# A W1 pair fetched ahead of the last WO rows and summed later, and a third attention block fetched ahead of the last x^T tiles, in a fused attention and MLP layer

## The chip, the cores and the metric

One core of a Trainium2 chip runs the whole program. The metric is the device time of one execution in microseconds (us). The kernel before took 1103.58 us (median of 3 runs, 1101.91 to 1105.1).

## The reference

`x` has 2048 rows of 576 numbers. After a layer norm without gain, an attention branch and an MLP branch read the same rows, and both are added to `x`:

```
xn = layernorm(x)
q, k, v = split(xn @ wqkv)                  # 32 heads of 18
logits = (q . k at s, s-2, ..., s-14) * 18 ** -0.5   # 8 keys, masked below row 0
A = (softmax(logits) @ v) @ wo              # wo: 576 x 576
B = maximum(xn @ w1, 0) @ w2                # w1: 576 x 4608, w2: 4608 x 576
return x + A + B
```

Everything is float32.

## The kernel before, in words

**Numbers.** Each matrix operand is split in two parts, a high part (`hi`, written by ScalarE) and a low part (`lo`, the difference, written by VectorE or GpSimd), and TensorE adds three products, hi*hi, hi*lo and lo*hi. The split is what most ScalarE and VectorE instructions do (`two`, L169, L171, L173; `ot_split`, L722 to L724; `xt_parts`, L429 to L435).

**Phases and groups.** The rows are worked on in two phases (even rows, then odd rows), each with four tiles of x^T of 256 rows (`XT[ph, 0..3]`). W1 has 36 blocks of 128 columns. Two blocks form a pair; for each pair and each two x^T tiles there is one group `g` (30 groups in phase 0, whose first 6 blocks are done in the opening, 36 in phase 1). A group multiplies 2 x 2 blocks by seven products (Strassen's scheme in Winograd's form, `M`, L1011), so sums of W1 blocks are needed (`sw_mix`, L977) and sums of x^T tiles (`ts_steps`, L444 to L470). The hidden values go through the ReLU (`c_parts`, L812 and L816) and are multiplied with W2 (`o_half`, tile `po`).

**Steps.** `group` is written out by hand as eight steps. A step gives TensorE one set of paired products and one half of an output piece. The events tied to a step are fired in its middle (`"T"`) or at its end (`"O"`); `on(ph, g, i, "O", f)` ties `f` to step `i`. Each engine takes its instructions strictly in the order written: one that waits holds up all that stand behind it on that engine. Within a group, step 2 copies bank `a` to bank `q` (`seed`, ScalarE L1045, tile `ph<-ph`), and TensorE needs that bank in step 4 (the rows `ph<-xS` that follow `pm<-xT`).

**W1.** For pair `p`, whose first group is `a = 2p`, `sw_load` (L965, L970, SyncE) fetches the four blocks into the staging tile `st` in step 4 of group `a - 2`, after the last splits of the pair before it have read `st`. Three sums (`sw_mix`) come in step 8 of `a - 2` and steps 1 and 2 of `a - 1`, the fourth in step 4, on VectorE in phase 1. The splits (`sw_prep`) follow from step 5 on.

**Where attention ends.** Attention is VectorE work spread over the groups, four units of eight heads a phase. The last unit's result goes to DRAM (`o_out`, L647, `od<-att`). Then the projection with WO needs: the last two of five groups of WO rows (`wo_rest`, L264 and L267, `att<-wo`), which land in the tile `att` that `od<-att` has just been read from; the four blocks of rows of the attention output (`ot_in`, L713 and L715, `att<-od`, block `r` = 0 to 3); and their splits (`ot_split`). These steps stand in a list (`ot_plan`) of entries with a condition and with ages in modelled TensorE time of earlier entries; `ot_go` takes the first entry that is ready, at places written in the groups. `ot_go(ph, r)` takes entries until block `r` is split.

**The seam.** `seam` joins the phases: `tail_pieces` ends phase 0's last group, and `more(k)` in it fetches the last x^T tiles of phase 1 (`xt_in`, L402 and L404, `xT<-words`, tiles 2 and 3); then blocks 0 and 1 are multiplied with WO (`wo_half`, L139, `po<-wq,att`), with the preparation of phase 1 taken from the list `side`. Blocks 2 and 3 are multiplied in the gaps of phase 1's first group (`prologue` and `wo_fill`). In phase 1, `epilogue` does the projection after the last group.

Of the kernel before, what the change touches and what calls it, by code (L numbers as in the profile page):

```python
# [66 lines left out]
def tile_body(ctx: ExitStack, tc: tile.TileContext, x, wqkv, wo, w1, w2, out):  # L67
# [14 lines left out]
    NP = [(NF - f) // 2 for f in F0]  # L82
    NG = [2 * n for n in NP]
# [39 lines left out]
    t = {"pe": 0.0, "dve": 0.0}  # L123
# [88 lines left out]
    def w2_load(ph, f):  # L212
        z = W2S[ph, f] = st2.tile([P, D], F32, name="st2")
        nc.sync.dma_start(z, w2[f * P : (f + 1) * P, :])
# [60 lines left out]
    hold = {}  # L275
# [124 lines left out]
    def words_in(z, td):  # L400

        nc.sync.dma_start(z[:, 0:KT], td[0 : KT * P].rearrange("(k p) t -> p k t", p=P))  # L402
        for part in LOW, UPP:
            nc.sync.dma_start(z[part, KT], td[KT * P : D])  # L404
# [14 lines left out]
    def xt_in(ph, tb):  # L419
        d = XT[ph, tb] = xtp.tile([P, 10, TBN], F32R, name="xT")  # L420
        words_in(f32(d[:, 0:5, :]), TD.pop((ph, tb)))
# [134 lines left out]
    ready = {}  # L556
# [545 lines left out]
    def on(ph, g, i, z, f, *a):  # L1102
        if g < 0:
            ph, g = ph - 1, g + NG[ph - 1]
        evs[ph, g, i, z].append((f, a))
# [5 lines left out]
    def plan_strassen(ph):  # L1111
        for p in range(NP[ph]):
            a = 2 * p
            f = F0[ph] + 2 * p
            engine = nc.vector if p > 1 or ph else nc.gpsimd
            if p or ph:
                on(ph, a - 2, 4, "O", sw_load, ph, p)
                for k, (d, i) in enumerate(((-2, 8), (-1, 1), (-1, 2)) if p > 1 or ph else ((-1, 3),) * 3):
                    on(ph, a + d, i, "O", sw_mix, k, engine)
                on(ph, a - 1, 4, "O", sw_mix, 3, engine)  # L1120
                on(ph, a - 1, 5, "T", sw_prep, ph, p, "A11")
                on(ph, a - 1, 5, "O", sw_prep, ph, p, "S2")
                on(ph, a - 1, 7, "T", sw_prep, ph, p, "S1", "A12")
                if p:
                    on(ph, a, 2, "O", sw_prep, ph, p, "S3", "S4")
                    on(ph, a, 3, "T", sw_prep, ph, p, "A22", "rem")
                if p:
                    on(ph, a - 1, 5, "O", w2_load, ph, f)
                    on(ph, a - 1, 6, "O", w2_load, ph, f + 1)
                on(ph, a, 6, "T", w2_split, ph, f, (0,), True)  # L1130
                on(ph, a, 8, "T", w2_split, ph, f, (1,), True)
                on(ph, a + 1, 1, "O", w2_split, ph, f + 1, (0,))
                on(ph, a + 1, 3, "O", w2_split, ph, f + 1, (1,))
        for u, g in QKV_G[ph].items():
            on(ph, g - (3 if u else 2), 4, "O", wq_load, ph, u)
            for kt, (d, i) in enumerate(((-2, 4 if u else 8), (-2, 7 if u else 8), (-1, 1), (-1, 4), (-1, 6))):
                on(ph, g + d, i, "O", wq_split, ph, u, kt)
            for tb in range(NTB):
                a, i = g + tb // 2, 3 + 4 * (tb % 2)
                ins[ph, a, i].append((qkv_half, (ph, u, tb, False, True)))  # L1140
                ins[ph, a, i + 1].append((qkv_half, (ph, u, tb, True, True)))
            on(ph, g + 2, 1, "T", halos, ph, u)
            on(ph, g + 2, 1, "T", attention, ph, u)
            if u:
                on(ph, g + 2, 4, "T", attention_rest, ph, u)
            else:
                on(ph, g - 2, 6, "O", zero_row, ph, K_ROW)
                on(ph, g - 1, 2, "O", zero_row, ph, V_ROW[0])
        g = QKV_G[ph][NU - 1] + 2
        on(ph, g, 1, "O", wo_first, ph)  # L1150
        on(ph, g + 1, 5, "O", wo_split, ph, 0)
        on(ph, g + 3, 3, "O", wo_split, ph, 1)
        on(ph, g + 5, 3, "O", wo_split, ph, 2)
        g = NG[ph] - 1
        if ph:
            on(ph, g, 5, "O", hold.__setitem__, ("xs", ph), True)
            on(ph, g, 1, "O", last_room, ph)
        else:
            on(ph, g, 4, "O", last_room, ph)
            on(ph, g, 4, "O", xt_in, 1, 0)  # L1160
            on(ph, g, 4, "O", hold.__setitem__, ("go", 0), True)
            on(ph, g, 4, "O", ot_go, 0)
            on(ph, g, 5, "O", xt_in, 1, 1)
            on(ph, g, 5, "O", hold.__setitem__, ("go", 1), True)
            for i in (6, 7, 8):
                on(ph, g, i, "O", ot_go, 0)

# [2 lines left out]
    def ot_plan(ph):  # L1170
        z = OTQ[ph] = []
        done = lambda: ph in ready and t["pe"] > ready[ph] + 4.5
        free = lambda: done() and ("xs", ph) in hold

        def go(r):
            if ph:
                return free if r == 3 else done
            return lambda: done() and ("go", r) in hold

        z.append(("wl", wo_rest, (ph,), lambda: ph in ready and t["pe"] > ready[ph] + 4.0, ()))  # L1180
        for kt in range(3, KT + 1):
            z.append((("ws", kt), wo_split, (ph, kt), None, (("wl", 11 + 3.0 * (kt - 3)),)))
        for r in range(4):
            z.append((("in", r), ot_in, (ph, r), go(r), ((("in", r - 1), 3.0),) if r else (("wl", 2.0),)))
            for h in range(2):
                z.append((("split", r, h), ot_split, (ph, r, h), None, ((("in", r), 12.0),)))

    def ot_go(ph, need=None):
        z = OTQ.get(ph, [])
        if need is not None:  # L1190
            todo_now = [("split", need, 0), ("split", need, 1), ("ws", KT)]
            while any((ph, k) not in OTT for k in todo_now):
                assert ot_one(ph, z, False), (ph, need)
            return
        ot_one(ph, z, True)

    def ot_one(ph, z, timed):
        for e in z:
            name, f, a, when, after = e
            if when is not None and not when():  # L1200
                continue
            if any((ph, k) not in OTT or timed and OTT[ph, k] + d > t["pe"] for k, d in after):
                continue
            z.remove(e)
            f(*a)
            OTT[ph, name] = t["pe"]
            return True
        return False
# [183 lines left out]
    def aside(n):  # L1392
        for _ in range(min(n, len(side))):
            f, *a = side.popleft()
            f(*a)

    def tail_pieces(ph, more, then):
        g = NG[ph] - 1
        tail_end(ph, more, lambda: (then(), o_half(ph, g, 2, False)))
        then()  # L1400
        own_banks(g, 3, ps_m, "pm", D - 256)
        o_half(ph, g, 3, False)
        then()
        for piece in (2, 3):
            o_half(ph, g, piece, True)
            o_evict(ph, g, piece)

    def sums(tp):
        side.extend([(ts_run, 1, tp, 1)] * 4)
        for i in range(4 * tp, 4 * tp + 4):  # L1410
            side.extend([(xt_parts, 1, i, 0), (xt_parts, 1, i, 1)])
        side.extend([(low_twin, 1, 2 * tp)] + [(ts_run, 1, tp, 1)] * 4)

    def seam():

        def more(k):
            ot_go(0)
            if k > 1:
                xt_in(1, k)

        tail_pieces(0, more, lambda: ot_go(0))
        hold["go", 2] = True
        for i in range(2):
            w2_load(1, i)
        sums(0)
        side.extend([(sw_prep, 1, 0, "S3", "S4"), (sw_prep, 1, 0, "A22", "rem")])
        for r in range(2):
            for k in range(4):
                ot_go(0, r) if k == 0 else ot_go(0)
                wo_half(0, r, k % 2, k > 1)  # L1430
                aside(3)
                if k == 2:
                    ot_go(0, r + 1)
            if r == 0:
                hold["go", 3] = True
        sums(1)
# [109 lines left out]
    late(22, sw_prep, 0, 0, "S3", "S4")  # L1546
    late(23, sw_prep, 0, 0, "A22", "rem")
    plan_strassen(0)
    plan_strassen(1)
    ot_plan(0)  # L1550
    ot_plan(1)

    both, x_low, w_low, last = TERMS[0:4], TERMS[4:8], TERMS[9:13], [TERMS[8], TERMS[13]]
# [92 lines left out]
    for n in range(FIRST, NOLD - 2):  # L1646
        g = n - n % 2 + LAG
# [17 lines left out]
    for g in range(1, NG[0]):  # L1665
        group(0, g)
    seam()
    prologue(1, wo_fill)
    for g in range(1, NG[1]):
# [29 lines left out]
```

## Time and profile before

| | before |
|---|---|
| runs, median (lowest to highest) | 1103.58 us (1101.91 to 1105.1) |
| profiled execution | 1107.0 us |
| its span, first to last instruction | 1105.2 us |
| TensorE (PE) busy | 1092.0 us, 99% |
| VectorE (DVE) busy | 844.1 us, 76% |
| ScalarE (ACT) busy | 590.8 us, 53% |
| GpSimd (POOL) busy | 274.1 us, 25% |
| moved by DMA | 179.62 MB, mean 163 GB/s |
| granted TensorE clock, mean | 0.997 |

The profile is one execution. A row of its timeline reads: start in us from the span's start, length in us, engine, line of the kernel, operation, tile written and tile read, shape, count; in brackets how long the engine had been idle before it, and what ended that. SPq rows are SyncE's DMA issues. A row of the chain of waits reads: who waited, for whom, us in total, times, longest. A row of busy time by stretch gives the stretch, its length, busy time of PE, PEld (weight loads), DVE, ACT and POOL, then the granted clock, the mean busy share of the 16 DMA engines and what they moved in GB/s. A row of DMA issues gives tiles, queue, count, KB each and the median us from issue to landing.

### The profile page before, as it was taken

How to read it: one execution, taken by the hardware profiler on the slowest of the kernel's cores; microseconds unless marked ns; L12 is line 12 of the kernel's file. 1: busy time of each engine (PE TensorE's matmuls, PEld its weight loads, DVE VectorE, ACT ScalarE, POOL GpSimd, SP SyncE). 2: the span in 40 equal slices, each digit the busy share in tenths (PEclk: the TensorE clock that was granted, in tenths of full speed). 3: DMA queues.
4: the chain of work that ended last, by engine and by line, in shares of the span. 5: the costliest groups of instructions: out<-in, count | busy, mean ns of one | idle time of the engine just before them, and what ended most of it. 6: DMA issues, size and time to landing. Idle time of an engine off the chain costs nothing.

```text
span 1105.2 us, 37855 instructions
## 1 busy us (share of the span) xinstructions
PE 1092.0 (99%) x16338; PEld 1081.9 (98%) x16338; DVE 844.1 (76%) x1402; ACT 590.8 (53%) x1396; POOL 274.1 (25%) x267
## 2 busy tenths in 40 slices
PE   9999999999999999999999999999999999999898
PEld 8999999999999999999999999999999999999898
DVE  7676888897997988893763297988889798896521
ACT  5433563564466366565774466356356446655640
POOL 2311521222222223322231122223022222223121
PEclk9999999999999999999999999999999999999899
DMA  7469995696597598889966597499579569888886
GB/s 231 138 163 226 189 195 95 147 207 108 122 223 132 90 219 158 157 157 259 239 139 122 107 205 142 76 218 172 91 157 205 101 132 205 155 165 177 192 135 149
DMA packets 138806, 179.62 MB, mean 163 GB/s; under 512 B 28032, under 2 KB 85120, under 8 KB 138608
## 3 DMA queue, kind: packets, MB, share of 16 engines
q0 software_dynamic: 38720, 83.76, 48.2%
q1 hardware_dynamic: 99200, 92.55, 29.4%
q8 instruction: 129, 2.11, 0.7%
q10 hardware_dynamic: 720, 0.89, 0.2%
q14 instruction: 37, 0.30, 0.1%
HBM read 74.07 MB, written 98.58 MB: 156 GB/s over the span
## 4 chain that ended last, share of the span: by engine, by line
PE 93%; DMA 4%; DVE 1%; SPq 1%; issue 1%; ACT 0%; POOL 0%; DVEq 0%; POOLq 0%; ACTq 0%
PE po L160 35%; PE po L139 19%; PE ph L160 18%; PE pm L160 14%; PE pm L139 2%; DMA st<-in_w 2%; PE ph L139 2%; PE ph L127 1%; DMA xT<-words 1%; PE po L127 1%; DMA att<-od 1%; SPq L398 1%; PE po L116 0%; PE pm L351 0%; DVE att L416 0%
## 5 line engine op out<-in xcount | busy, mean ns | idle before, releaser
L160 PE MATMUL po<-ar 64*128 64x256 f32 (+1 forms) x6240 | 498.4, 289 | 0.0
L160 PEld LDWEIGHTS po<-ar 64*128 64x128 f32 x6240 | 435.3, 184 | 0.4 <-PE ph L160 0.4
L160 PE MATMUL ph<-xT,ar 64*128 64x256 f32 x2772 | 348.8, 274 | 0.2 <-DVE ar L816 0.2
L160 PEld LDWEIGHTS ph<-xT,ar 64*128 64x128 f32 x2772 | 314.7, 185 | 0.7 <-DVE ar L816 0.4
L771 POOL DMA_DIRECT2D out<-ev x131 | 157.4, 1202 | 547.4 <-ACT ev L765 408.3
L160 PE MATMUL pm<-xS,ar 64*128 64x256 f32 x2376 | 282.5, 274 | 0.0
L160 PEld LDWEIGHTS pm<-xS,ar 64*128 64x128 f32 x2376 | 259.7, 184 | 0.3
L765 ACT ACTIVATE ev<-po 128x512 f32<-128x512 f32 (+1 forms) x272 | 176.8, 652 | 115.5 <-PE po L160 83.1
L173 DVE TENSOR_TENSOR ar<-st,ar 128x256 fp32r<-128x256 f32 (+3 forms) x244 | 128.9, 548 | 46.8 <-ACT ar L169 46.3
L139 PE MATMUL po<-wq,xT 64*128 64x432 f32 x1512 | 156.4, 354 | 0.0
L169 ACT ACTIVATE ar<-st 128x256 fp32r<-128x256 f32 (+3 forms) x314 | 150.6, 500 | 4.9 <-DMA st<-in_w 2.7
L139 PEld LDWEIGHTS po<-wq,xT 64*128 64x128 f32 x1512 | 138.4, 184 | 4.6
L160 PE MATMUL ph<-xS,ar 64*128 64x256 f32 x792 | 113.5, 277 | 6.1 <-ACT ph L1045 6.1
L160 PEld LDWEIGHTS ph<-xS,ar 64*128 64x128 f32 x792 | 104.9, 186 | 6.8 <-ACT ph L1045 6.6
L171 POOL TENSOR_TENSOR ar<-st,ar 128x256 fp32r<-128x256 f32 (+1 forms) x70 | 75.9, 1085 | 143.5 <-ACT ar L169 101.8
L618 DVE TENSOR_TENSOR pr<-att 128x1152 f32<-128x1152 f32 x64 | 88.3, 1392 | 0.4
L583 DVE TENSOR_TENSOR pr<-att 128x1152 f32<-128x1152 f32 x64 | 87.0, 1369 | 0.1
L586 DVE TENSOR_REDUCE att<-pr 128x64 f32<-128x1152 f32 x64 | 85.8, 1344 | 0.0
L977 DVE TENSOR_TENSOR st<-st 128x256 f32<-128x256 f32 x128 | 62.6, 490 | 14.9 <-DMA st<-in_w 14.7
L541 ACT ACTIVATE att<-po 128x288 f32<-128x288 f32 (+1 forms) x88 | 28.7, 403 | 81.2 <-PE po L139 81.2
L625 DVE TENSOR_TENSOR pr<-pr 128x1152 f32<-128x1152 f32 x64 | 69.2, 1082 | 1.4
L160 PE MATMUL pm<-xT,ar 64*128 64x256 f32 x396 | 67.5, 276 | 0.1
(131 smaller groups left out, 1218.5 us busy)
## 6 DMA issues: line engine op xcount, KB each, us to landing
out<-ev POOLq DMA_DIRECT2D x131, 576.0 KB, 7.1
st<-in_w SPq DMA_DIRECT2D x72, 288.0 KB, 5.2
st<-in_w SPq DMA_DIRECT2D x69, 256.0 KB, 3.7
att<-att SPq DMA_DIRECT2D x16, 441.0 KB, 4.6
att<-in_wqkv SPq DMA_DIRECT2D x28, 216.0 KB, 6.8
od<-att SPq DMA_DIRECT2D x32, 160.0 KB, 6.5
st<-in_w SPq DMA_DIRECT2D x66, 64.0 KB, 6.4
att<-in_x SPq DMA_DIRECT2D x14, 288.0 KB, 4.1
```

Source lines behind the costliest of these rows:

```text
L139: ins = nc.tensor.matmul(o, l[z], r[z], start=start, stop=stop)
L160: b.ins = nc.tensor.matmul(b.ap, l[part], r[part], start=start, stop=stop, skip_group_check=skip)
L169: nc.scalar.activation(hi, src, AF.Copy)
L171: nc.gpsimd.tensor_tensor(lo, src, f32(hi), op=ALU.subtract)
L173: nc.vector.tensor_tensor(lo, src, f32(hi), op=ALU.subtract)
L583: nc.vector.tensor_tensor(pr[i], q, window(k, i), op=ALU.mult)
L586: nc.vector.tensor_reduce(lg[:, i], pr.pop(i).rearrange(heads, d=Dh), axis=AX.X, op=ALU.add)
L618: nc.vector.tensor_tensor(pr[i].rearrange(heads, d=Dh), e, window(v, i).rearrange(heads, d=Dh), op=ALU.mult)
L625: nc.vector.tensor_tensor(o, z[:, :, 0:n], z[:, :, n : 2 * n], op=ALU.add)
L765: nc.scalar.activation(acc[:, :, cols], z[:, :, 0 : cols.stop - cols.start], AF.Copy)
L771: ADDED[ph, tb] = nc.gpsimd.dma_start(rows_of(ph, tb), acc, accum_op=ALU.add)
L977: engine.tensor_tensor(stg(o), stg(a), stg(b), op=op)
```

## The change

```
             if p or ph:
                 on(ph, a - 2, 4, "O", sw_load, ph, p)
-                for k, (d, i) in enumerate(((-2, 8), (-1, 1), (-1, 2)) if p > 1 or ph else ((-1, 3),) * 3):
+                if (ph, p) in ((1, 0), (1, NP[1] - 1)):
+                    on(ph, a - 2, 4, "O", hold.__setitem__, ("wl", 1 if p else 0), True)
+                apart = p and a + 2 < NG[1] if ph else p > 1
+                for k, (d, i) in enumerate(((-2, 8), (-1, 1), (-1, 2)) if apart else ((-1, 3),) * 3):
                     on(ph, a + d, i, "O", sw_mix, k, engine)
...
             on(ph, g, 5, "O", hold.__setitem__, ("go", 1), True)
+            on(ph, g, 6, "O", hold.__setitem__, ("go", 2), True)
...
-        z.append(("wl", wo_rest, (ph,), lambda: ph in ready and t["pe"] > ready[ph] + 4.0, ()))
+        z.append(("wl", wo_rest, (ph,), lambda: ph in ready and t["pe"] > ready[ph] + 4.0 and ("wl", ph) in hold, ()))
...
-            z.append((("in", r), ot_in, (ph, r), go(r), ((("in", r - 1), 3.0),) if r else (("wl", 2.0),)))
+            z.append((("in", r), ot_in, (ph, r), go(r), ((("in", r - 1), 6.0 if ph else 3.0),) if r else (("wl", 2.0),)))
...
             if k > 1:
                 xt_in(1, k)
+            if k == 3:
+                ot_go(0, 0)
 
         tail_pieces(0, more, lambda: ot_go(0))
-        hold["go", 2] = True
```

Only in phase 1's first and last pair do the first three W1 sums move: all three now stand in step 3 of group `a - 1`. The WO rows of a phase wait, in the order of the program, until that pair's load has been written. In phase 1 the blocks of attention rows are written at least 6 us of modelled time apart instead of 3. In phase 0 block 2 may be fetched from step 6 of the last group on, and block 0 is split by the end of `more(3)`.

SyncE at the end of attention in phase 1, before: `st` is the W1 staging tile, `wo2` the WO rows, `od` the attention output in DRAM, `st2` W2 rows.

```order
L647 DMA od_12469<-att_11326 32x5x256 x4
L264 DMA att_20292<-wo2_143 128x576
L267 DMA att_20292<-wo2_143 64x1x576 x2
L965 DMA st_82<-in_w1 128x2x256 x2
L970 DMA st_82<-in_w1 64x2x128 x2
L713 DMA att_20292<-od_12469 128x4x256
```

The same place now:

```order
L647 DMA od_12469<-att_11326 32x5x256 x4
L965 DMA st_82<-in_w1 128x2x256 x2
L970 DMA st_82<-in_w1 64x2x128 x2
L264 DMA att_20354<-wo2_143 128x576
L267 DMA att_20354<-wo2_143 64x1x576 x2
L713 DMA att_20354<-od_12469 128x4x256
```

The W1 load has moved ahead of the two WO issues that stood between it and `od<-att`. (In phase 0 it stood ahead of them already.)

VectorE at the same place, before: `u3` and `m5` are sums of the hidden values of the group before, `st` the W1 sums.

```order
L1054 TENSOR_TENSOR u3_20448<-u3_20448,pm_20276 128x256
L977 TENSOR_TENSOR st_82<-st_82 128x2x128
L1054 TENSOR_TENSOR m5_20387<-m5_20387,ph_20257 128x256
L816 SCALAR_TENSOR_TENSOR ar_72<-u3_20448,ar_72 128x256
L816 SCALAR_TENSOR_TENSOR ar_72<-m5_20387,ar_72 128x256
L173 TENSOR_TENSOR ar_72<-st2_20148,ar_72 128x256
L977 TENSOR_TENSOR st_82<-st_82 128x2x128 x2
```

And now:

```order
L1054 TENSOR_TENSOR u3_20448<-u3_20448,pm_20276 128x256
L1054 TENSOR_TENSOR m5_20384<-m5_20384,ph_20257 128x256
L816 SCALAR_TENSOR_TENSOR ar_72<-u3_20448,ar_72 128x256
L816 SCALAR_TENSOR_TENSOR ar_72<-m5_20384,ar_72 128x256
L173 TENSOR_TENSOR ar_72<-st2_20148,ar_72 128x256
L173 TENSOR_TENSOR ar_72<-st2_20148,ar_72 128x320
L977 TENSOR_TENSOR st_82<-st_82 128x2x128 x3
```

The first sum no longer stands between `u3` and `m5`; all three stand behind the W2 splits. The end of phase 0 changes in the same way.

SyncE at the seam, before: `words` holds x^T in DRAM; the first four rows are x^T tiles 2 and 3, then come two W2 rows, and the last two rows are block 2 (block 1 stands just ahead of this piece).

```order
L402 DMA xT_10458<-words_1801 128x4x256
L404 DMA xT_10458<-words_1801 64x256 x2
L402 DMA xT_10475<-words_2160 128x4x256
L404 DMA xT_10475<-words_2160 64x256 x2
L214 DMA st2_10573<-in_w2 128x576
L214 DMA st2_10575<-in_w2 128x576
L713 DMA att_10055<-od_1876 128x4x256
L715 DMA att_10055<-od_1876 64x1x256 x2
```

And now, with block 2 in the first two rows (block 1 still just ahead of them):

```order
L713 DMA att_10055<-od_1876 128x4x256
L715 DMA att_10055<-od_1876 64x1x256 x2
L402 DMA xT_10461<-words_1801 128x4x256
L404 DMA xT_10461<-words_1801 64x256 x2
L402 DMA xT_10478<-words_2160 128x4x256
L404 DMA xT_10478<-words_2160 64x256 x2
L214 DMA st2_10576<-in_w2 128x576
L214 DMA st2_10578<-in_w2 128x576
```

Block 2 is now issued ahead of x^T tiles 2 and 3 and of two W2 rows; block 3 (not shown) stays behind them.

## The prediction

> **What bounds the kernel now.** I read the page first, then who TensorE waits for, then its timeline at those waits, then the engines behind them.
>
> ```profile
> PE 1092.0 (99%) x16338; PEld 1081.9 (98%) x16338; DVE 844.1 (76%) x1402; ACT 590.8 (53%) x1396; POOL 274.1 (25%) x267
> ```
>
> TensorE is the bound; only its waits, and the clock lost in them, can be won. The chain of waits:
>
> ```profile
> PE ph L160 <- ACT ph L1045: 6.1, 2, 4.8
> PE po L139 <- DVE att L723: 0.6, 2, 0.4
> ```
>
> Two waits for the copy into bank `q` make up 6.1 us, one of them 4.8. TensorE's timeline around it:
>
> ```profile
> 1012.30 0.28 PE L160 MATMUL pm<-xT,ar 64*128 64x256 f32 x1
> ...
> 1023.98 0.28 PE L160 MATMUL pm<-xT,ar 64*128 64x256 f32 x1
> 1029.07 0.58 PE L160 MATMUL ph<-xS,ar 64*128 64x256 f32 x1 [4.81 <-ACT ph L1045]
> ...
> 1043.23 0.28 PE L160 MATMUL pm<-xT,ar 64*128 64x256 f32 x1
> ```
>
> The `pm<-xT` rows are step 4 of three groups in a row. The first interval is 11.68 us, an undisturbed group; the second is 19.25. This group loses 7.57 us: the wait, and a slow stretch behind it. The busy time by stretch shows why (granted clock third from the end):
>
> ```profile
> 1028.00:1029.00 1.00, 0.00 (x0) 0.00 (x0) 0.85 (x3) 0.98 (x4) 0.00 (x0) 0.50 1.12 316
> ...
> 1034.00:1035.00 1.00, 1.00 (x18) 1.00 (x18) 0.85 (x2) 0.67 (x2) 0.00 (x0) 0.81 0.92 232
> ```
>
> The clock had fallen to 0.50 in the wait and came back only after 1034. So 7.57 - 4.81 = 2.76 us is the price of the clock. VectorE, then ScalarE:
>
> ```profile
> 1011.52 1.29 DVE L173 TENSOR_TENSOR ar<-st,ar 128x512 fp32r<-128x512 f32 x2 [1.34 <-ACT ar L169]
> ...
> 1019.44 0.42 DVE L1054 TENSOR_TENSOR u<-u,pm 128x256 f32<-128x256 f32 x1 [2.35 <-ACT u L1049]
> 1027.23 0.43 DVE L977 TENSOR_TENSOR st<-st 128x256 f32<-128x256 f32 x1 [7.37 <-DMA st<-in_w]
> 1027.57 0.41 DVE L1054 TENSOR_TENSOR m<-m,ph 128x256 f32<-128x256 f32 x1
> ```
>
> ```profile
> 1028.02 0.42 ACT L812 ACTIVATE ar<-m 128x256 fp32r<-128x256 f32 x1 [7.70 <-DVE m L1054]
> ...
> 1028.65 0.36 ACT L1045 ACTIVATE ph<-ph 128x256 f32<-128x256 f32 x1
> ```
>
> VectorE sits 7.37 us on the first W1 sum (L977); `m` behind it is late, ScalarE's L812 waits for `m`, and the copy that TensorE needs stands behind L812. SyncE shows why the load was late:
>
> ```profile
> 1008.12 1.81 SPq L647 DMA_DIRECT2D od<-att  x4
> 1016.97 0.34 SPq L264 DMA_DIRECT2D att<-wo  x1
> ...
> 1018.63 1.76 SPq L965 DMA_DIRECT2D st<-in_w  x2
> 1020.44 1.31 SPq L970 DMA_DIRECT2D st<-in_w  x2
> ```
>
> ```profile
> SPq L264 <- DMA od<-att: 6.9, 1, 6.9
> ```
>
> The WO issue waits 6.9 us for `od<-att` to be out of the tile, and the W1 load waits behind it though `st` was free from 1012.81, when the splits at 1011.52 ended.
>
> **The change part by part.**
>
> *Load and sums of the last pair.* The load is now directly behind `od<-att` and can go at 1012.85 instead of 1018.63, 5.8 us earlier. Its price in time to land is best read where the same order already stood, at the end of phase 0 (first issue of `st` at 497.67):
>
> ```profile
> 497.67 1.15 SPq L965 DMA_DIRECT2D st<-in_w  x2
> ...
> 507.64 0.43 DVE L977 TENSOR_TENSOR st<-st 128x256 f32<-128x256 f32 x1 [3.85 <-DMA st<-in_w]
> ```
>
> It was there by 507.6, 9.9 us after the first issue: here 1022.8. The sums now stand in step 3, which TensorE leaves at 1023.98, and behind a split that ScalarE feeds; so I expect no wait. Were the load a few us late, `u`, `m`, their ReLU parts and the copy stand ahead of it; behind the sums stand a ReLU part wanted four steps on (some 5.8 us by 11.68 / 8 a step) and the splits for the group that starts after 1030. Two covers for one wait: I take all 7.57 us, with a lower end of 4.81 if a new wait shorter than 2.76 us comes behind.
>
> *Sums of the first pair.* At the end of phase 0 only the sums move. TensorE there:
>
> ```profile
> 496.22 0.28 PE L160 MATMUL pm<-xT,ar 64*128 64x256 f32 x1
> ...
> 496.91 0.94 PE L160 MATMUL po<-ar 64*128 64x256 f32 x12
> ...
> 507.90 0.28 PE L160 MATMUL pm<-xT,ar 64*128 64x256 f32 x1
> ...
> 510.17 0.94 PE L160 MATMUL po<-ar 64*128 64x256 f32 x12
> ```
>
> Step 4's products took 0.69 us in the one group and 2.27 in the next: 1.58 us lost. VectorE now reaches the sums as the load lands (507.6); nothing that TensorE needs soon stands behind. Gain 1.58 us, lower end 0.
>
> *Block 2 at the seam.* TensorE's first half of block 2 lies between the first two of these rows; the next two enclose an undisturbed half of the same width:
>
> ```profile
> 542.21 0.28 PE L160 MATMUL ph<-xT,ar 64*128 64x256 f32 x1
> ...
> 546.33 0.27 PE L160 MATMUL pm<-xS,ar 64*128 64x256 f32 x1
> ...
> 549.09 0.28 PE L160 MATMUL ph<-xT,ar 64*128 64x256 f32 x1
> ...
> 551.32 0.28 PE L160 MATMUL ph<-xS,ar 64*128 64x256 f32 x1
> ```
>
> 4.12 us against 2.23, of which 0.11 is for one pair of products more: 1.78 us lost. It waits for the splits, and those for data:
>
> ```profile
> 514.51 1.38 SPq L713 DMA_DIRECT2D att<-od  x1
> ...
> 530.06 0.38 SPq L713 DMA_DIRECT2D att<-od  x1
> ```
>
> ```profile
> 542.63 1.36 ACT L722 ACTIVATE att<-att 128x640 fp32r<-128x640 f32 x2 [0.15 <-DMA att<-od]
> ```
>
> ```profile
> att<-od SPq DMA_DIRECT2D x1, 512.0 KB, 12.0
> ```
>
> Block 2 was issued at 530.06, 15 us after block 1, and landed 12.0 us later. Now it follows block 1, at about 517; even at 12.0 us it lands by 530. Its two splits go in among the x^T splits and the cuts of `xS`, which ScalarE and VectorE then finish one or two splits (0.7 and 1.0 us each) later; by my count of these rows VectorE ends the second split 0.6 us before TensorE wants it. Gain 1.78, lower end 0; 0.4 us off for that thin margin. Block 0's earlier split costs nothing: it lies ahead of evictions that wait for TensorE anyway. The passed tiles and W2 rows come under the rivals.
>
> *Wider spacing and later WO rows in phase 1.* Both are wanted only behind the last group, in the epilogue; I price them at nothing unless the WO rows hold ScalarE (below).
>
> *Sum.* 7.57 + 1.58 + 1.78 - 0.4 = 10.5 us against the profiled 1107.0: 1096.5. That execution is 3.4 us above the median of the runs, 1103.58. If the runs lose as much as it did, the median becomes 1093.1; if their 3.4 us less is a smaller loss, they end where it would, at 1096.5. I take 1094.0, nearer the first: start and end differ between executions as well.
>
> The end of phase 0 shows what a short wait does to the clock:
>
> ```profile
> 508.00:509.00 1.00, 0.18 (x4) 0.00 (x0) 0.85 (x4) 0.57 (x2) 0.00 (x0) 1.00 1.06 228
> ```
>
> It stayed at 1.00 in a wait of 1.3 us. The Trainium skill, "TensorE: Matmul & The Clock Gate", section on the HAM clock gate, puts the step to half rate after an idle window of about 3.4 us and the step back after about 3.4 us of work. The trace agrees on the first (TensorE stops at 1024.26, 0.50 by 1028) and not on the second (over 5 us of slow work from 1029.07); by the page the clock would cost 1.7 us and not 2.76, and the sum 9.4.
>
> **The rivals.**
>
> *The runs lose less.* Their spread of 3.2 us is about the clock's price. Where the wait is under about 3 us the clock stays: at most 3 + 1.58 + 1.78 = 6.4 us are to be won, 1097.2. For it: the profiled execution is the longest of all. Against: the load is issued 5.8 us late in every run.
>
> *WO rows hold ScalarE.* They now queue behind the W1 load.
>
> ```profile
> att<-wo SPq DMA_DIRECT2D x1, 288.0 KB, 8.3
> ```
>
> In phase 0, in this order, they took 8.3 us: here landed at 1025.3, just as ScalarE comes to their split in step 5. Behind it stand evictions of `po` that TensorE wants within a step or so. Each us beyond some 1027 costs one, and past 3 the clock's 2.76: landing at 1034, 17 us after issue, gives back 5.5 + 2.76 and leaves 1101.3, no change. Against: none of the rows is that slow.
>
> *Slower: x^T tile 3 comes too late.*
>
> ```profile
> xT<-words SPq DMA_DIRECT2D x1, 512.0 KB, 15.0
> ...
> 522.97 2.39 SPq L404 DMA_DIRECT2D xT<-words  x2
> ...
> 545.49 1.29 DVE L470 TENSOR_TENSOR pr<-xT 128x512 f32<-128x512 f32 x2
> ...
> 520.00:525.00 5.00, 5.00 (x72) 4.82 (x72) 1.07 (x2) 1.64 (x4) 1.20 (x1) 1.00 1.12 273
> ```
>
> Block 2, 640 KB at 273 GB/s, is 2.3 us of transfer put ahead of tiles 2 and 3. Tile 3's issues end at 525.4; at 15.0 us each the last rows land between 538 and 540, say 539, and it is wanted at 545.49: 6.5 us to spare. Less 2.3, and 3.4 for a TensorE that is earlier there, leaves 0.8. Past that VectorE holds, in L470, everything for phase 1's first groups. To end slower by 0.3%, 10.5 + 3.3 us must go, so 11 us of wait plus the clock: tile 3 would have to take 27 us; then 1107. For it: the engines are full here (share 1.12).
>
> The Trainium skill, "DMA: Bandwidth & Descriptors", section on queues, rings and completion order, speaks for this case: all of SyncE's transfers use one ring per DMA engine and are taken in ring order, so the moved block holds up all that it passes, by its whole length. That is the 2.3 us, and not 11.
>
> **How the numbers follow.** The forecast, all three waits gone, 1091 to 1096: 0.62. Smaller loss in the runs, 1096 to 1099.5: 0.26. WO rows late, no change: 0.07. Tile 3 late, slower: 0.05. The range 1091.0 to 1099.0 leaves out the last two and little more. 0.3% is 3.3 us, about what a measurement of this kernel can tell from no change; so faster (below 1100.3) 0.88, same 0.07, slower 0.05.
>
> **What would show it.** Right: L977's 7.37 us wait gone, SyncE's W1 issue near 1013 and ahead of WO, the clock 1.00 through the end of phase 1, group intervals of 11.68 us there, no wait of `po` L139 for L722 or L723 after block 1, and a profiled time near 1096.5. Wrong: a new wait of TensorE of over 1 us in the last two groups or the seam, ScalarE waiting for `att<-wo`, VectorE's L470 waiting for `xT<-words`, or a median above 1099 with all three waits gone.

## The result, and the profile after

The changed kernel took 1096.31 us (median of 6 runs, 1095.38 to 1096.8) beside 1103.62 us for the kernel before (6 runs, 1101.91 to 1106.48): ratio 0.9929, 95% interval 0.9915 to 0.9942, so 7.3 us faster. The profiled execution after took 1096.31 us, where the one before took 1107.0: 10.7 us less. Why one difference is 7.3 and the other 10.7 is the main question of what follows.

The span and the busy times, and who TensorE still waits for (total, times, longest):

```profile
span 1094.5 us, 37854 instructions
...
PE 1088.3 (99%) x16338; PEld 1078.5 (99%) x16338; DVE 845.2 (77%) x1402; ACT 590.1 (54%) x1396; POOL 273.0 (25%) x267
```

```profile
PE po L116 <- POOL mhalf L111: 1.4, 1, 1.4
PE ph L127 <- ACT xT L356: 0.7, 1, 0.7
PE pm L160 <- ACT u L1049: 0.2, 1, 0.2
```

The first two rows are the start of the program. The 6.1 us for the copy (L1045) and the waits of `po` (L139) for the attention splits are gone; in their place stands one wait of 0.2 us.

**End of attention in phase 1.** TensorE in step 4 of three groups, then the busy time by stretch (clock third from the end):

```profile
1009.24 0.28 PE L160 MATMUL pm<-xT,ar 64*128 64x256 f32 x1
...
1020.92 0.28 PE L160 MATMUL pm<-xT,ar 64*128 64x256 f32 x1
...
1032.60 0.28 PE L160 MATMUL pm<-xT,ar 64*128 64x256 f32 x1
```

```profile
1024.00:1029.00 5.00, 5.00 (x86) 5.00 (x84) 3.83 (x8) 4.61 (x12) 0.00 (x0) 1.00 1.09 294
1029.00:1036.00 7.00, 7.00 (x120) 7.00 (x119) 5.21 (x12) 5.41 (x13) 2.33 (x2) 1.00 1.04 256
```

Both intervals are 11.68 us, TensorE is busy without a gap and the clock stays at 1.00: the 19.25 us group is an ordinary one. The row at 1009.24 answers to the one at 1012.30 before: 3.06 us had been won by then, and 7.57 more came here. SyncE, how long its W1 loads took to land, and VectorE:

```profile
1005.05 1.79 SPq L647 DMA_DIRECT2D od<-att  x4
1009.18 2.47 SPq L965 DMA_DIRECT2D st<-in_w  x2
1011.71 1.92 SPq L970 DMA_DIRECT2D st<-in_w  x2
1014.41 0.35 SPq L264 DMA_DIRECT2D att<-wo  x1
```

```profile
st<-in_w SPq DMA_DIRECT2D x2, 256.0 KB, 7.3
...
st<-in_w SPq DMA_DIRECT2D x2, 64.0 KB, 7.2
```

```profile
1022.22 0.49 DVE L173 TENSOR_TENSOR ar<-st,ar 128x320 fp32r<-128x320 f32 x1 [2.86 <-ACT ar L169]
1022.63 1.33 DVE L977 TENSOR_TENSOR st<-st 128x256 f32<-128x256 f32 x3
1023.89 0.41 DVE L816 SCALAR_TENSOR_TENSOR ar<-pm,ar 128x256 fp32r<-128x256 f32 x1
```

The load goes 4.1 us after `od<-att`, ahead of WO. The rows on landing give the median of two pieces; the last piece alone, issued at 1012.36, took 7.1 us and was there at about 1019.5, so the sums at 1022.63 had some 3 us to spare and waited for nothing.

**End of phase 0 and seam.** TensorE's step 4 in the group that had lost time, then its first half of block 2; SyncE's issue of block 2 and the time it took to land; VectorE's second split of it:

```profile
507.72 0.28 PE L160 MATMUL pm<-xT,ar 64*128 64x256 f32 x1
...
508.40 0.84 PE L160 MATMUL po<-ar 64*128 64x256 f32 x12
...
540.69 0.28 PE L160 MATMUL ph<-xT,ar 64*128 64x256 f32 x1
...
541.38 1.46 PE L139 MATMUL po<-wq,att 64*128 64x256 f32 x22
...
543.04 0.28 PE L160 MATMUL pm<-xS,ar 64*128 64x256 f32 x1
```

```profile
518.13 0.37 SPq L713 DMA_DIRECT2D att<-od  x1
```

```profile
att<-od SPq DMA_DIRECT2D x1, 512.0 KB, 11.8
```

```profile
539.22 0.68 DVE L723 TENSOR_TENSOR att<-att 128x512 fp32r<-128x512 f32 x1
539.94 0.29 DVE L724 TENSOR_TENSOR att<-att 64x128 fp32r<-64x128 f32 x1
```

Step 4 takes 0.68 us where it took 2.27, block 2's half 2.35 where it took 4.12. Block 2's large piece lands at 529.9; VectorE ends its second split at 540.23, 1.15 us before TensorE begins the half at 541.38.

### The profile page after: what moved, and what is told of

Same layout as the page of the kernel before. It is cut to its first block, busy times and chain, and to the rows that moved or that the text cites. A ratio compares the mean times of both kernels' runs of the same rounds, so it can differ in the third digit from the quotient of the medians.

```text
span 1094.5 us, 37854 instructions
## 1 busy us (share of the span) xinstructions
PE 1088.3 (99%) x16338; PEld 1078.5 (99%) x16338; DVE 845.2 (77%) x1402; ACT 590.1 (54%) x1396; POOL 273.0 (25%) x267
## 4 chain that ended last, share of the span: by engine, by line
PE 97%; ACT 1%; DMA 1%; DVE 0%; issue 0%; POOL 0%; DVEq 0%; ACTq 0%; POOLq 0%; SPq 0%
PE po L160 36%; PE po L139 21%; PE ph L160 18%; PE pm L160 15%; PE pm L139 2%; PE ph L139 2%; PE ph L127 1%; PE po L127 1%; DMA st<-in_w 1%; PE po L116 0%; PE pm L351 0%; ACT ar L169 0%; DVE st L977 0%; PE pm L127 0%; ACT ev L765 0%
## 5 line engine op out<-in xcount | busy, mean ns | idle before, releaser
L160 PE MATMUL po<-ar 64*128 64x256 f32 (+1 forms) x6240 | 492.1, 288 | 0.0
L160 PEld LDWEIGHTS po<-ar 64*128 64x128 f32 x6240 | 429.0, 184 | 0.5 <-PE ph L160 0.4
L139 PE MATMUL po<-wq,xT 64*128 64x432 f32 x1512 | 156.6, 354 | 0.0
L139 PEld LDWEIGHTS po<-wq,xT 64*128 64x128 f32 x1512 | 138.4, 184 | 4.8 <-ACT ev L765 0.2
```

Of the source, the lines that this page charges most:

```text
L139: ins = nc.tensor.matmul(o, l[z], r[z], start=start, stop=stop)
L160: b.ins = nc.tensor.matmul(b.ap, l[part], r[part], start=start, stop=stop, skip_group_check=skip)
```

## The experiments

Each run is compared with runs of the kernel before on the same chip. Those came in three sets, with medians of 1106.7 (34 runs), 1106.2 (20) and 1106.9 us (17), against 1103.6 in the first comparison. The executions of one kernel differ among themselves, on each of the three chips on which the sets were taken. All 71, by mean granted clock, beside the 6 of the changed kernel:

| mean granted clock | runs | mean, us | lowest to highest |
|---|---|---|---|
| before, 1.000 | 12 | 1101.8 | 1101.1 to 1102.4 |
| before, 0.998 | 18 | 1103.9 | 1101.9 to 1106.9 |
| before, 0.997 | 26 | 1107.4 | 1104.6 to 1110.0 |
| before, 0.995 | 15 | 1108.9 | 1107.5 to 1111.2 |
| after, 0.999 and 1.000 | 6 | 1096.1 | 1095.4 to 1096.8 |

The profiled execution of before (1107.0, 0.997) is one of the largest group. The mean clock counts slow stretches: each window at half rate (3.41 us, last section) costs about 1.7 us and lowers the mean over 1102 us by 0.0015, so 0.998, 0.997 and 0.995 stand for one, two and three. The profiles agree for the first two: none at 1.000 (the load alone, below), one at 0.998 (the last pair alone), two at 0.997 (before); none at 0.995 was profiled. By this estimate some 5.1 of the 7.1 us between the first group and the last are the clock, and the rest are longer waits. Whether the chip has a part in how often the clock falls is not shown; one of the three had no run of before at 1.000 among its 17.

**The last pair alone** (load and sums):

```
+                if (ph, p) == (1, NP[1] - 1):
+                    on(ph, a - 2, 4, "O", hold.__setitem__, ("wl", 1), True)
+                apart = a + 2 < NG[1] if ph else p > 1
...
+  ... and (ph == 0 or ("wl", ph) in hold)      # wo_rest
```

> Last pair of phase 1 alone: its load ahead of the WO rows and its three sums in step 3 (blocks of attention rows still 3 us apart in modelled time). If the waits are separate: in the trace the two groups around 1024 take 11.68 us each, 7.6 us less than before, the seam's waits (1.3 us for bank q and about 0.8 us for block 2) stay, profiled time about 1099.4 to 1100. In the runs, if they lose less there than the profiled execution did, 3.5 to 5 us less than before; if they lose as much, 7.6 us less. If the waits are coupled (a wait removed comes back later): below 3 us in the trace.

1099.92 us (12 runs), ratio 0.9958, 0.9937 to 0.9979. No wait of TensorE around 1024, clock 1.00 there. What remains is the seam, here with a clock that fell (TensorE's waits, then the busy time by stretch):

```profile
542.57 0.38 PE L139 MATMUL po<-wq,att 64*128 64x256 f32 x1 [0.58 <-ACT att L722]
...
544.34 1.73 PE L139 MATMUL po<-wq,att 64*128 64x256 f32 x13 [0.40 <-DVE att L723]
```

```profile
544.00:545.00 1.00, 0.66 (x6) 0.66 (x8) 0.94 (x3) 0.00 (x0) 0.97 (x2) 0.76 1.18 256
545.00:546.00 1.00, 1.00 (x13) 1.00 (x12) 1.00 (x3) 0.00 (x0) 0.77 (x1) 0.50 1.03 195
```

Three short waits, 1.23 us in all with the one of 0.25 between these, brought the clock to 0.50 until about 548. In the first profile of before the same three waits, 0.92 us in all (0.25, 0.25, 0.42), left it at 1.00.

**The load alone, the sums alone.** The first has the two lines on `hold` and `wo_rest`, the second only the line `apart`.

> Last pair's load ahead of the WO rows, its sums where they were. If an earlier load is enough: it lands near 1022.8, VectorE waits about 3 us on the first sum, TensorE under 1 us, the clock stays 1.00, 6.5 to 7.5 us less than before in the trace. If the place of the sums decides: TensorE still waits 3 us or more and the clock falls.

1099.32 us (11 runs), ratio 0.9945, 0.9927 to 0.9962. The sum in its old place waited only 1.22 us on VectorE and nothing of that reached TensorE:

```profile
1021.70 0.76 DVE L977 TENSOR_TENSOR st<-st 128x256 f32<-128x256 f32 x1 [1.22 <-DMA st<-in_w]
```

> Last pair's sums in step 3, its load still behind the WO rows. If the place of the sums is enough by itself (they stand behind all that TensorE wants soon): no wait of TensorE, 7.6 us less in the trace. If what stands behind the sums matters after all (ReLU part of bank r, then the copy into r that TensorE wants in step 7): VectorE waits to about 1027.2 and TensorE about 1 us in step 7, without loss of clock, 6 to 6.6 us less. If the late load itself decides: a wait of 3 us or more.

1101.8 us (12 runs), ratio 0.997, 0.9951 to 0.9989. The load, issued at 1019.16, was there for the sums at 1025.96, and the long wait was gone. Smaller ones came later, 0.56 us at 1033.54 and this one, from somewhere else (ScalarE, then TensorE):

```profile
1036.32 0.74 ACT L722 ACTIVATE att<-att 128x640 fp32r<-128x640 f32 x1 [2.84 <-DMA att<-od]
...
1037.58 0.36 ACT L1045 ACTIVATE ph<-ph 128x256 f32<-128x256 f32 x1
```

```profile
1038.00 0.38 PE L160 MATMUL ph<-xS,ar 64*128 64x256 f32 x1 [0.95 <-ACT ph L1045]
```

ScalarE stands 2.84 us at a block of attention rows, with the copy behind it. So either cover is enough for the 4.8 us wait; the load is the better one, since the blocks of attention rows stand behind it on SyncE. Both together (1099.92 us) gave no more than the load alone (1099.32).

**The seam alone, the first pair alone.** The first has the three lines on `("go", 2)` and `ot_go(0, 0)`, the second:

```
+                apart = p if ph else p > 1
```

> Block 2 ahead of the x^T tiles 2 and 3, block 0 split earlier; nothing else. If the waits are separate: TensorE's waits for L722 and L723 gone, 1.78 us less in the trace around 543, the wait of 1.3 us at 508 and of 4.8 us at 1024 as before; 1.3 to 2.0 us less in the runs. If x^T tile 3 is now late: VectorE waits at L470 and TensorE gains under 1 us.

1101.76 us (12 runs), ratio 0.997, 0.9949 to 0.9991. The waits of `po` L139 for L722 and L723 are gone. But in its profile (1106.26 us) most of the gain is given back at the next wait (VectorE, TensorE):

```profile
1027.52 0.43 DVE L977 TENSOR_TENSOR st<-st 128x256 f32<-128x256 f32 x1 [9.77 <-DMA st<-in_w]
```

```profile
1029.35 0.58 PE L160 MATMUL ph<-xS,ar 64*128 64x256 f32 x1 [7.21 <-ACT ph L1045]
```

TensorE came 2.1 us earlier to that group than before (step 4 at 1021.87, not 1023.98), and waited 2.4 us longer.

> The kernel before with only the first pair's three sums in one step (end of phase 0); load, WO order, last pair and seam as before. My theory: TensorE's wait for the copy near 508 (1.3 us) goes and with it 1.58 us, the sums stand there without a wait for the load; but near the end of phase 1 the last pair's load is bound to land at about the same absolute time (1027.4 in the last run in which only the seam was changed), so the wait there grows by about what was won ahead of it, from 4.8 to some 6.4 us, and the runs' median falls by 0 to 0.8 us. Rival, that the three parts are independent and add up: the wait there stays at 4.8 us and the median falls by 1.6 us, ratio 0.9986.

1106.68 us (12 runs), ratio 1.0006, 0.9983 to 1.0029: no gain, as my theory had it, though not in the way it said. The wait near 508 was gone, but the one near 1028 was 2.62 us and not 6.4: this time the load landed 6 us after its issue, where it had taken 8.6. So "the load lands at the same absolute time" fell. The clock took the rest (TensorE, busy time by stretch):

```profile
1028.01 0.38 PE L160 MATMUL ph<-xS,ar 64*128 64x256 f32 x1 [2.62 <-ACT ph L1045]
```

```profile
1028.00:1029.00 1.00, 0.99 (x16) 0.99 (x18) 0.94 (x3) 1.00 (x3) 0.00 (x0) 1.00 1.08 351
1029.00:1030.00 1.00, 1.00 (x16) 1.00 (x15) 0.76 (x1) 1.00 (x4) 0.07 (x1) 0.66 1.11 370
1030.00:1031.00 1.00, 1.00 (x14) 1.00 (x13) 0.97 (x3) 0.27 (x1) 1.00 (x1) 0.50 1.12 316
```

It fell 1.3 us after work had begun again, and stayed down until 1032.7; at the seam (waits of 1.54 us) it fell too. 8 of the 12 runs were at 0.997 or lower.

**Tile 3 later.** The changed kernel with the last x^T tile behind the two W2 rows, and then behind block 3 too:

```
-            if k > 1:
+            if k == 2:
                 xt_in(1, k)
...
+        xt_in(1, 3)        # behind the W2 rows; or at the end of the loop over blocks 0 and 1
```

> The changed kernel with the last x^T tile fetched behind the two W2 rows instead of ahead of them (as if a second block had been moved ahead of it). The W2 rows take 1.8 us of issue and carry 576 KB, by the seam's 270 GB/s 2.1 us. My theory by the prediction's slack (0.8 us): VectorE waits 1 to 2 us at its first sum of x^T tiles 2 and 3 (near 542.7), TensorE 0.5 to 1.5 us in the first groups of phase 1, the median rises to 1097 to 1098. Rival, that the slack is 2 us or more since the moved block did not make the tile late at all: no wait there, median as the changed kernel, 1096.3.

> The changed kernel with the last x^T tile fetched behind the W2 rows and behind block 3 too, so from some 539.5 instead of 525.7: 13.8 us late. My theory: it lands near 549 to 551, VectorE waits 6 to 8 us at its first sum of tiles 2 and 3, all of it reaches TensorE in the first groups of phase 1 and the clock steps down for some us: profiled span 6 to 11 us above the changed kernel's 1094.5, median 1102 to 1107, which would give back all that the change won. Rival, that VectorE and ScalarE have work enough ahead (banks and sums of other tiles) to hide half of it: span 2 to 4 us above.

1096.81 us (6 runs, ratio to before 0.9923, 0.9899 to 0.9948) and 1096.04 us (6 runs, 0.9926, 0.9898 to 0.9954): both as fast as the changed kernel, and VectorE waits in neither for `xT<-words`. The second, SyncE and the time to land, then VectorE:

```profile
539.89 0.38 SPq L402 DMA_DIRECT2D xT<-words  x1
```

```profile
xT<-words SPq DMA_DIRECT2D x1, 512.0 KB, 5.1
```

```profile
545.90 1.28 DVE L470 TENSOR_TENSOR pr<-xT 128x512 f32<-128x512 f32 x2
```

Issued 14.2 us later than in the changed kernel (525.73), the tile's large piece landed only 5.1 us later (539.9 by its 14.2 us there, 545.0 here); 1.3 us of both are this whole execution, which was that much later at 516. My theory fell, and so did the rival, which still had 2 to 4 us. The profiled execution was the one long run of the six (1101.31), for another reason:

```profile
536.95 0.74 ACT L722 ACTIVATE att<-att 128x640 fp32r<-128x640 f32 x1 [1.71 <-DMA att<-od]
```

```profile
538.33 3.14 PE L139 MATMUL po<-wq,att 64*128 64x320 f32 x22 [1.94 <-ACT ev L765]
```

Block 2 took 16.1 us to land instead of 11.8, though nothing that was edited stands ahead of it; ScalarE waits at its split, an eviction stands behind, TensorE loses 1.94 us and the clock is at 0.50 until 542.

**Spacing of 3 us in phase 1.**

```
-  (("in", r - 1), 6.0 if ph else 3.0)
+  (("in", r - 1), 3.0)
```

> The changed kernel with the blocks of attention rows of phase 1 fetched 3 us of modelled time apart again instead of 6. The prediction priced the spacing at nothing: median 1096.3, ratio to the changed kernel 1.000, no wait of TensorE over 0.3 us after 1030. Rival, from the run with the sums alone, where ScalarE stood 2.84 us at the split of a block of attention rows with the copy behind it: with 3 us that split stands ahead of the copy here too, TensorE waits 0.5 to 1.5 us near 1035, the median rises by 1 to 1.5 us.

1097.52 us (9 runs, 1095.34 to 1102.08; ratio 0.994, 0.9915 to 0.9965). Its profile (span 1093.6) shows no wait of TensorE after 515. Two of the 9 runs were at 0.997 and 1102, which none of the 6 of the changed kernel was; no profile caught one. So the spacing costs nothing to undo in most executions, and whether it keeps out a few bad ones stays open.

**Late load, everything else as changed.** The lines on `("wl", ...)` are taken out:

```
-                if (ph, p) in ((1, 0), (1, NP[1] - 1)):
-                    on(ph, a - 2, 4, "O", hold.__setitem__, ("wl", 1 if p else 0), True)
```

> The changed kernel, but with the last pair's W1 load behind the WO rows again (its sums stay in step 3, the spacing stays 6 us). My theory, that both covers were needed since the load lands at 1026 to 1027.5 whatever was won before it: VectorE waits 3 to 5 us for the load at the sums, the ReLU part, the copy and the W1 splits behind them are late, TensorE waits 1 to 3 us within the next group, the clock falls in some executions; median 1098 to 1101. Rival, that the sums' new place is enough by itself and the waits in the run with the sums alone came from the attention blocks' spacing: no wait of TensorE over 0.3 us after 1020, median 1096 to 1097.

1098.95 us (6 runs, 1095.72 to 1101.85; ratio 0.9927, 0.9905 to 0.9949). The median is in my range, the mechanism is not mine: VectorE did not wait at the sums (1022.99, load issued at 1016.43). The block of rows behind the late load was late (ScalarE, TensorE):

```profile
1028.29 0.74 ACT L722 ACTIVATE att<-att 128x640 fp32r<-128x640 f32 x1 [0.93 <-DMA att<-od]
```

```profile
1031.09 0.38 PE L160 MATMUL pm<-xS,ar 64*128 64x256 f32 x1 [1.08 <-ACT u L1049]
```

This is the kind of wait that the run with the sums alone showed, in spite of the spacing of 6 us: ScalarE stood 0.93 us instead of 2.84, and TensorE lost about as much (1.08, there 0.95). Three of the 6 runs were at 0.998.

**Late WO rows** (10 us later in modelled time, splits in about the same place):

```
-  t["pe"] > ready[ph] + 4.0
+  t["pe"] > ready[ph] + (14.0 if ph else 4.0)
```

> The changed kernel with phase 1's WO rows (and with them the blocks of attention rows behind them) issued 10 us of modelled time later, the splits of WO at about the same place in ScalarE's order as now. My theory by the prediction's rival on WO rows (each us of landing beyond 1027 costs one, beyond 3 us the clock too): issued near 1024, landed near 1031 to 1033, ScalarE waits 6 to 8 us at the first split, TensorE 4 to 6 us, clock at 0.50 for some 3 us: median 1101 to 1105. Rival, that the evictions behind the split are not wanted that soon: TensorE waits under 1 us, median 1096 to 1097.5.

1097.49 us (10 runs, 1096.36 to 1103.71; ratio 0.9931, 0.991 to 0.9952). The edit gave no dose at all. The issue stands at 1017.38 and not at 1014.41, but this whole execution was 3.35 us later by then (step 4 of TensorE at 1012.59, not 1009.24): behind `od<-att` the WO rows came after 9.0 us, in the changed kernel after 9.4. SyncE's order is the same in both, and in both it waits there for `od<-att` to be out of the tile. What moved was the first split, 3.8 us earlier against TensorE's step 4, so that ScalarE waited

```profile
1024.55 0.69 ACT L169 ACTIVATE wq<-att 128x576 fp32r<-128x576 f32 x1 [0.58 <-DMA att<-wo]
```

0.58 us, of which TensorE saw nothing (no wait after 1005). The price of late WO rows was thus not measured, and neither theory nor rival was put to the test. Three runs were at 0.997 and 1102 to 1104; the profile does not show why.

**The kernel before, twice more.**

> The kernel before, unchanged, profiled once more, to see how its loss differs between executions. My theory, from the granted clocks and times of its runs (about 1101.1 to 1102.8 us at a mean clock of 1.000, 1107 to 1110 at 0.995 to 0.997): the waits at the end of attention and at the seam are there in every execution, but what differs is whether the clock falls behind them; an execution near 1102 shows the wait for the copy near 1029 at about 3 us or less and no stretch at 0.50, so loses 5 to 6.5 us in all against the changed kernel; one near 1107 shows 0.50 for 3 to 5 us at one or both places. Rival, as the prediction's number assumed: the loss at the three places is 10 us in every execution and what differs is start and end, so that an execution near 1102 shows the same 4.8 us wait and slow stretch as the first profile.

> The same kernel before, once more: as for the look ahead of it. By my theory the time of this execution is within 1.5 us of 1096 plus the TensorE time lost at the end of phase 0, at the seam and near 1029, clock included; by the rival it is not, and the difference lies in the first 20 or last 60 us.

1106.81 and 1110.09 us, both at a mean clock of 0.997. The first (TensorE, busy time by stretch):

```profile
1028.69 0.58 PE L160 MATMUL ph<-xS,ar 64*128 64x256 f32 x1 [4.98 <-ACT ph L1045]
```

```profile
1029.00:1036.00 7.00, 7.00 (x76) 7.00 (x76) 4.21 (x10) 4.36 (x12) 1.20 (x1) 0.61 1.09 288
```

Wait and slow stretch as in the first profile: at 0.61 in 7 us, 7 x 0.39 = 2.7 us of work are lost. The other waited 6.06 us there. They are the second and the third profile of before. The sums that my theory asked for, with the changed kernel's times as the undisturbed ones (step 4 of 0.68 us, a half of 2.35, a group of 11.68):

| profile of before | end of phase 0 | seam | end of attention in phase 1, with the clock | time less the sum |
|---|---|---|---|---|
| first | 1.59 | 1.77 | 7.57 | 1107.0 - 10.93 = 1096.07 |
| second | 0.76 | 2.24 | 7.97 | 1106.81 - 10.97 = 1095.84 |
| third | 1.31 | 2.16 | 8.51 | 1110.09 - 11.98 = 1098.11 |

The second is within my 1.5 us of 1096, the third is not. Its 1.9 us more were lost before 496 (step 4 at 497.81 there, at 495.93 in the second), 0.4 of them in the first 20 us and most of the rest in waits of 0.74 and 0.45 us near 141 and 166, so the rival did not have the place either. No execution near 1102 was profiled, so what it looks like inside is inferred from the table by clock alone.

## Why the prediction came out as it did

**Direction, mechanism and range: right; the number 2.3 us too low.** 1096.31 lies in 1091 to 1099, but just inside the stretch given to the rival of a smaller loss (1096 to 1099.5, 0.26) and not in the favoured one (1091 to 1096, 0.62). The signs named for "right" are in the trace: W1's issue ahead of WO (at 1009.18, the whole execution being 3.06 us earlier there), 11.68 us intervals, clock 1.00, no wait of L139, a profiled time of 1096.31 where 1096.5 was named.

**Load and sums of the last pair, 7.57 us: right in size.** The interval went from 19.25 to 11.68. From its first issue the load took 10.3 us to its last piece, where I had read 9.9. Of the "two covers" each alone removed the long wait. The second was thinner than I wrote: behind the sums stands L816 at 1023.89, and ScalarE's copy into the other bank waits for it.

```profile
1024.39 0.37 ACT L1045 ACTIVATE pm<-ph 128x256 f32<-128x256 f32 x1 [1.93 <-DVE ar L816]
```

```profile
1027.12 0.27 PE L160 MATMUL pm<-xT,ar 64*128 64x256 f32 x1
```

It ends at 1024.76 and TensorE's `pm<-xT` products come at 1027.12: at most 2.4 us to spare, not 5.8. With the 3 us by which the load was early, one some 5.6 us later would have reached TensorE, by this estimate; no run tried it.

**First pair, 1.58 us: right** (2.27 to 0.68). **Block 2, 1.78 less 0.4: right in size** (4.12 less 2.35 is 1.77); the margin of 0.6 us was 1.15, so the 0.4 was not needed in this execution. That it can run out is shown by the run with tile 3 behind block 3, where block 2 took 4.3 us longer to land and TensorE lost 1.94 us and the clock.

**The terms taken one by one do not add up.** I summed them as if independent. Alone, the first pair gave nothing (0.9983 to 1.0029), though its wait was gone: in its profile the clock took the gain back behind later waits. The seam alone gave 0.3% (0.0009 to 0.0051), some 3 us and more than its 1.8, though in its profile the long wait behind it took most of the gain back. The last pair alone gave 0.4%. Together they are worth the sum, because the last wait is gone.

**The mis-sized step: from the profile to the runs.** The sum of 10.5 us is right for an execution like the profiled one: 1107.0 to 1096.31. I then had two readings for the runs' median, the same loss in every run (1093.1) or one common floor (1096.5), and took 1094.0, "nearer the first: start and end differ between executions as well". The second reading was the right one, to 0.2 us. The table shows it: executions of before range over 10 us, ordered by their granted clock, and the 6 of the changed kernel all stand at 1095.4 to 1096.8. Against that floor an execution of before loses 5.7 us where the clock held, 7.8 where it fell for one window and 11 to 13 for more. The floor rests on 6 executions: of the 21 of its three near copies (tile 3 later, twice, and the spacing of 3 us), 3 stood at 0.997 or 0.998 and 1101 to 1102, so such executions of the changed kernel are not excluded. The first 3 runs of before happened to lie in the lower part; beside the experiments, where 41 of 71 lay in the two upper groups, the medians stood 9.9 to 10.6 us above 1096.3. Start and end do differ (TensorE is busy for 16.1 to 18.0 us of the first 20 in these profiles), but that scatter is under 2 us.

**The rivals.** "The runs lose less" was on the right side of the number, 0.9 us high with its 1097.2, and right that the clock is what differs; its condition, that the clock stays in a wait under about 3 us, was not (it fell behind 2.62 and 1.94). WO rows: ScalarE's first split came at 1024.98 without a wait. The working of that rival was out as well: landing at 1034 is 7 us beyond 1027, which at one us each is not 5.5, so by its own terms it leaves some 1102.8 and not 1101.3. Tile 3: no wait at L470 either. The "0.8 us to spare" came from giving the tile 15.0 us to land wherever it is issued; the two runs with tile 3 later show that the time to land shrinks by most of the delay.

**The clock rule: I read it wrongly.** The prediction held the Trainium skill, "TensorE: Matmul & The Clock Gate", section on the HAM clock gate, against the row and found that it did not agree with the way back to full rate, since over 5 us of slow work followed the long wait. The runs agree with the page: the clock changes in whole windows (last section), the long wait had cost two of them at half rate, and the first of these began while TensorE was still idle; only the second was busy throughout, and at its end the clock came back. The price of 2.76 us, taken from the row, was the right one.

## What to carry to other kernels

When one kernel's runs spread over more than their usual noise, order them by granted clock before choosing what the profile is compared with: here the change that removed the waits removed most of the spread as well, so its time was the common floor, and that was the profiled time less the loss seen in that profile, not the median less it. Add to waits of TensorE that come to about 1.2 us and more within a few us the 1.7 us that the clock may cost behind them, and price several waits in a row as one chain: what an early one gives is kept only if no later wait hangs on a transfer. A margin for a transfer is not its usual time to land added to its issue; here a transfer moved back by 14.2 us in a full queue landed 5.1 us later.

## What the runs showed of the hardware

**The clock falls in windows of 3.41 us, and behind short waits too.** From the share of half rate in the first and last row of each slow stretch its ends can be worked out. In the first profile of before:

```profile
1027.00:1028.00 1.00, 0.00 (x0) 0.00 (x0) 0.77 (x3) 0.00 (x0) 0.00 (x0) 0.78 1.09 368
```

A mean of 0.78 is 0.44 us at 0.50, so the clock fell at 1027.56; the row at 1034 (0.81, 0.38 us) puts the return at 1034.38. In the run with the first pair alone, near 1029 (first row shown there: 0.66, so 1029.32) and at the seam:

```profile
544.00:545.00 1.00, 0.74 (x8) 0.74 (x10) 0.94 (x3) 0.00 (x0) 1.00 (x2) 0.81 0.96 174
548.00:549.00 1.00, 1.00 (x18) 1.00 (x16) 0.00 (x0) 0.98 (x3) 0.00 (x0) 0.98 1.08 216
...
1032.00:1033.00 1.00, 1.00 (x15) 1.00 (x14) 0.85 (x3) 0.57 (x2) 0.00 (x0) 0.64 1.05 297
```

| kernel | waits, us | clock at 0.50 | length, us |
|---|---|---|---|
| last pair alone, seam | 1.23 | 544.52 to 547.92 | 3.40 |
| first pair alone, seam | 1.54 | 544.62 to 548.02 | 3.40 |
| tile 3 behind block 3, seam | 1.94 | 538.56 to 541.96 | 3.40 |
| first pair alone, end | 2.62 | 1029.32 to 1032.72 | 3.40 |
| before, end | 4.81 | 1027.56 to 1034.38 | 6.82 |
| before, second profile, end | 4.98 | 1027.64 to 1034.48 | 6.84 |
| seam alone, end | 7.21 | 1025.72 to 1032.56 | 6.84 |

The length is one or two times 3.41 each time, within the 0.02 us of such a reading, and the two falls with the first pair alone lie 484.70 us apart, 142 times 3.413. The fall behind the last product fits too: with the last pair alone the row from 1097 to 1098 (0.74) puts it at 1097.48, 552.96 us or 162 windows after the one at 544.52. So the windows run on by themselves through the whole program. The Trainium skill, in the same section, says that the window is 4096 cycles, 3413 ns, and free-running; the trace agrees to the hundredth. It does not agree that a whole window must be idle: behind 1.23 us of waits the clock fell. Counted back from the falls, 1.35 us of waits at the seam of the second profile of before lay on both sides of a window's edge (542.95: 0.69 ahead of it, 0.66 behind), and so did 1.30 us near 508 in the first (edge at 508.73); at both the clock held. So where the edge falls, which differs from one execution to the next, bears on whether one and the same wait costs 1.7 us more. It does not decide it alone: in the run with late WO rows TensorE stood 1.33 us in one piece inside one window (929.09 to 932.50, counted in windows from 4.08, where this trace's record of the clock begins), and the clock held.

```profile
930.72 0.38 PE L160 MATMUL ph<-xS,ar 64*128 64x256 f32 x1 [1.33 <-ACT ph L1045]
```

That window held 35 products; the one ahead of the fall with the last pair alone (541.10 to 544.51) held 26, in three waits of 1.23 us together, and an undisturbed one holds 60. What the clock goes by, and where its limit lies, is therefore open; longest wait and sum of waits are not enough to tell.

The place of the edge is one reason for the ten microseconds over which the runs of before spread; that it is the only one is argued, not shown, since no execution at 1.000 was profiled.

**The same W1 load took from 6 to 10 us** to be there for the sums (first pair alone: issued 1020.06, summed 1026.18; seam alone: 1017.05 and 1027.52), with the same order of issues around it, counted from the first issue. What decides it was not found.

**A transfer issued later behind the same backlog landed in less time.** Tile 3's 512 KB took 14.2 us when issued at 525.73, 9.8 at 532.69 and 5.1 at 539.89. The Trainium skill, "DMA: Bandwidth & Descriptors", section on queues, rings and completion order, has the transfers of one issuer taken in ring order on each DMA engine; the three runs agree, but they do not single it out, since what else was under way at those times differs too.
